# Gram products put into the recurrence's visits, and four inverse steps behind each h, in a DeltaNet and SwiGLU kernel

## The chip, the cores and the metric

The kernel runs on one core of one Trainium2 chip. The metric is the device time of one execution in microseconds (us). The core has five engines that run beside each other and wait for each other through semaphores: PE (matmuls, with its weight loads shown as PEld), DVE (vector work), ACT (activations and copies), POOL (a few general operations) and SP (it issues most DMAs).

## The reference

Two parts, one behind the other, all in float32. The first is a delta rule over 4 batches and 8 heads, 768 tokens, head size 48:

```python
k_n = k / (np.linalg.norm(k, axis=-1, keepdims=True) + 1e-06)
for t in range(S):
    kt, vt, bt = (k_n[:, :, t], v[:, :, t], beta[:, :, t, None])
    y[:, :, t] = np.einsum('bhd,bhde->bhe', q[:, :, t], state)
    v_old = np.einsum('bhde,bhd->bhe', state, kt)
    state = state + bt[:, :, :, None] * np.einsum('bhd,bhe->bhde', kt, vt - v_old)
```

Then y, as 3072 tokens of 384 numbers, goes through a SwiGLU block with d_ff = 1536: `(silu(x @ w_gate) * (x @ w_val)) @ w_out`.

## The kernel before

**Chunks and stages.** The 768 tokens are cut into 12 chunks of 64. The recurrence (chunk c needs the state that chunk c-1 left) and the FFN run at the same time: while PE works on the FFN of chunk c, the small matmuls of chunk c+1's recurrence are put between its big ones. The FFN of one chunk from chunk 2 on is called *stage c* here. It consists of six gate/value pairs (`gate_val`, f = 0, 2, ..., 10; line 847: 6 matmuls of p_gate, 6 of p_val, on full 128 x 128 tiles) and of the output product (from chunk 3 = `FAST` on `output_fast`, line 959, which saves one of eight quarter products by sums and differences of h). After each pair ACT makes silu, DVE multiplies it into h (line 862), and in the later three pairs `sums_of_h` (lines 917 and 944) makes sums of rows that the output product reads.

**The recurrence of a chunk** is `advance(c)`, in four steps: (1) v scaled, then p_r = kt x state, p_y = qt x state, and v minus p_r on DVE (line 759); (2) p_u = inverse x v, copied to uu by ACT; (3) p_s, the new state (added on DVE, line 803), and p_y completed, copied to y; (4) p_f, the transposition of y for the FFN. Steps 1 to 3 use 64 x 64 tiles, in groups of 64 rows of the trace.

**Its preparation** is made ahead. `turned(c, of_q)` transposes k or q of a chunk on DVE (kt, qt, line 422) and sends for the next chunk's blocks by DMA. `gram` multiplies them (line 444); DVE copies the k gram to a_sb and the masked q gram to p_sb. When both k grams of a pair g of chunks (2g, 2g+1) are there, `invert(g)` is entered in a list `fills`. It is a sequence of small DVE steps: three transposes of mb (lines 477, 480), a power on POOL (line 655) during which the sequence yields `WAIT` twice, some scaling, 31 substitution steps of two dependent instructions each (lines 510 and 516), and transposes into zt and z1. `join(g)` completes the inverse with two products on PE with 32 x 32 tiles (lines 706 and 720), with ACT and DVE copying between and behind.

**Order.** The program order of each engine is written out by the kernel's own Python loops, and each engine works its queue in that order:

```python
        for c in range(2, NCH):
            for f in range(0, FT, 2):
                point(c + 1)
                gate_val(c, f, fill)
            point(c + 1)
            ...
                output_fast(c, fill)
            ...
            finish(c + 1)
```

`point` is a place for a *visit*: a run of small-tile matmuls between the big ones. Before, it takes either a step of `advance`, or, in `prep_step`, a join step, or the transposes of the next chunks, or, one point later, their grams (`products`: k of one chunk and q of another in one visit). `fill(n)` runs n steps of the list `fills`: 2 behind p_gate, 3 behind each h, and 2, 2 and 7 within and behind the output product.

**PSUM.** The pair tags "px" and "py" hold one two-bank tile each, for all of the recurrence; the tag "ffn" has four banks, which p_gate, p_val and p_o take in turn.

## Time and profile before

| | us |
|---|---|
| median of 8 runs | 738.91 (738.03 to 741.15) |
| the profiled execution | 739.28 |
| its span on the core | 737.6 |
| PE busy, DVE busy | 698.0, 472.9 |
| stage 4 (305.6 to 362.6) | 57.0 |
| stage 5 (362.6 to 416.6) | 54.0 |

A profile's row gives a start in us from the span's start, a duration, the engine, the source line, and what is written from what, with partitions x elements; a number in brackets is the engine's idle time before it and what ended it. Matmuls overlap, so the distance from one start to the next is what a group costs. Up to about 205 us the kernel also converts the FFN's weights on DVE; behind that the stages repeat in pairs, the even ones with an inverse and the odd ones without. The granted clock over the span was 0.968, and 1.00 in the stages.

### The profile page before, as it was taken

What the parts mean: (1) busy time and instruction counts of PE and PEld (TensorE: products, weight loads), DVE (VectorE), ACT (ScalarE), POOL (GpSimd) and SP (SyncE); (2) the same over time, 40 slices, a digit from 0 to 9 for tenths busy, and PEclk for the clock granted to TensorE, in tenths of its full rate; (3) what the DMA queues carried; (4) which work ended last, traced back from release to release, by engine and by line L of the source; (5) the groups of instructions that cost most, each with busy time, mean ns of one, the idle gap of its engine ahead of it and who ended that gap; (6) DMA issues with size and microseconds to landing.
All of it is one profiled execution on the core that took longest, in us unless ns stands there. A gap on an engine that the chain in (4) does not pass through costs nothing.

```text
span 737.6 us, 22478 instructions
## 1 busy us (share of the span) xinstructions
PE 698.0 (95%) x10132; PEld 605.0 (82%) x10132; DVE 472.9 (64%) x977; ACT 154.6 (21%) x287; POOL 66.4 (9%) x46
## 2 busy tenths in 40 slices
PE   4748899999999999999999999999999999999997
PEld 3636788866787788988988988988988988989987
DVE  5999988978498163678854678854578853313122
ACT  3555444302401112011012011012011012021010
POOL 7008100201200000030000030000030000000000
PEclk9556999999999999999999999999999999999999
DMA  7775444121231012331302331302310100100000
GB/s 149 188 222 139 124 108 127 39 40 24 56 43 26 22 24 42 48 67 14 53 3 46 42 58 26 52 3 38 48 28 12 33 3 3 23 3 0 22 1 21
DMA packets 130735, 37.18 MB, mean 50 GB/s; under 512 B 122864, under 2 KB 125936, under 8 KB 130640
## 3 DMA queue, kind: packets, MB, share of 16 engines
q1 hardware_dynamic: 127184, 34.01, 23.0%
q10 hardware_dynamic: 3072, 1.57, 1.0%
q8 instruction: 79, 1.29, 0.7%
q0 software_dynamic: 384, 0.17, 0.2%
q14 instruction: 16, 0.13, 0.1%
HBM read 31.01 MB, written 4.72 MB: 48 GB/s over the span
## 4 chain that ended last, share of the span: by engine, by line
PE 82%; DVE 14%; issue 1%; DMA 1%; ACT 0%; SPq 0%; ACTq 0%; DVEq 0%
PE p_gate L847 23%; PE p_val L847 23%; PE p_o L959 17%; PE p_o L876 6%; DVE tmp L510 3%; PE p_g L444 3%; DVE zb L516 3%; PE p_u L763 2%; PE p_r L742 1%; PE p_s L794 1%; PE p_y L782 1%; PE p_y L751 1%; DVE last_h L287 1%; DMA kn<-in_k_dram 1%; DVE h_f L862 1%
## 5 line engine op out<-in xcount | busy, mean ns | idle before, releaser
L847 PE MATMUL p_gate<-x_ffn,wg_sb 128*128 128x256 f32 x864 | 205.3, 388 | 1.5 <-ACT x_ffn L830 1.5
L847 PE MATMUL p_val<-x_ffn,wv_sb 128*128 128x256 f32 x864 | 198.5, 379 | 0.0
L847 PEld LDWEIGHTS p_val<-x_ffn,wv_sb 128*128 128x128 f32 x864 | 163.8, 190 | 22.3
L847 PEld LDWEIGHTS p_gate<-x_ffn,wg_sb 128*128 128x128 f32 x864 | 161.6, 192 | 24.4 <-ACT x_ffn L830 2.0
L862 DVE TENSOR_TENSOR h_f<-sil,p_val 128x512 f32<-128x512 f32 x71 | 48.5, 683 | 147.6 <-PE p_val L847 147.2
L856 ACT ACTIVATE sil<-p_gate 128x512 f32<-128x512 f32 x72 | 43.0, 597 | 277.3 <-PE p_gate L847 251.1
L655 POOL TENSOR_TENSOR n_b<-mb,half 128x32 f32<-128x32 f32 x5 | 43.3, 8662 | 409.4 <-DVE mb L480 368.2
L959 PE MATMUL p_o<-wo_sb,h_f 128*128 128x192 f32 x432 | 75.6, 328 | 0.1
L959 PEld LDWEIGHTS p_o<-wo_sb,h_f 128*128 128x128 f32 x432 | 70.3, 190 | 1.2 <-DVE o_sb L969 0.7
L510 DVE TENSOR_TENSOR tmp<-zb,mb 128x31 f32<-128x31 f32 (+15 forms) x186 | 63.2, 340 | 12.1 <-PE p_j L630 6.8
L516 DVE TENSOR_TENSOR zb<-zb,tmp 128x31 f32<-128x31 f32 (+15 forms) x186 | 63.7, 342 | 6.6 <-DVE tmp L510 0.2
L969 DVE TENSOR_TENSOR o_sb<-o_sb,p_o 128x192 f32<-128x192 f32 x45 | 15.7, 349 | 53.4 <-PE p_o L959 36.2
L876 PE MATMUL p_o<-wo_sb,h_f 128*128 128x384 f32 x136 | 45.7, 490 | 0.0
L876 PEld LDWEIGHTS p_o<-wo_sb,h_f 128*128 128x128 f32 x136 | 25.4, 190 | 16.5
L959 PE MATMUL p_o<-last_k,h_f 128*128 128x192 f32 x180 | 32.2, 326 | 0.0
L959 PEld LDWEIGHTS p_o<-last_k,h_f 128*128 128x128 f32 x180 | 29.7, 190 | 0.0
L917 DVE TENSOR_TENSOR h_f<-h_f,h_f 128x256 f32<-128x256 f32 x54 | 22.4, 424 | 8.0 <-PE p_o L959 7.1
L959 PE MATMUL p_o<-last_h,h_f 128*128 128x192 f32 x144 | 26.3, 326 | 0.0
L959 PEld LDWEIGHTS p_o<-last_h,h_f 128*128 128x128 f32 x144 | 23.9, 190 | 0.0
L254 ACT ACTIVATE last_h<-last_h,rebias 128x512 int32<-128x512 uint32 (+2 forms) x26 | 15.3, 616 | 30.5 <-DVE last_h L246 30.5
L763 PEld LDWEIGHTS p_u<-vin,zt 64*64 64x64 f32 x768 | 13.7, 141 | 6.9 <-issue 3.2
L763 PE MATMUL p_u<-vin,zt 64*64 64x48 f32 x768 | 15.7, 228 | 2.4 <-DVE vin L759 1.2
(180 smaller groups left out, 689.2 us busy)
## 6 DMA issues: line engine op xcount, KB each, us to landing
vin<-in_v_dram SPq DMA_DIRECT2D x96, 48.0 KB
kn<-in_k_dram SPq DMA_DIRECT2D x40, 96.0 KB
out_dram<-o_sb SPq DMA_DIRECT2D x36, 96.0 KB
zt<-in_moe_w_out_dram SPq DMA_DIRECT2D x6, 384.0 KB
staged<-in_moe_w_out_dram SPq DMA_DIRECT2D x6, 384.0 KB
qpad<-in_q_dram SPq DMA_DIRECT2D x36, 64.0 KB
wo_sb<-in_moe_w_gate_dram SPq DMA_DIRECT2D x4, 512.0 KB
wo_sb<-in_moe_w_val_dram SPq DMA_DIRECT2D x4, 512.0 KB
```

The costliest lines, as they stand in the source:

```text
L444: nc.tensor.matmul(p_v[par][half_of(b if of_q else b ^ par), bp, j], kt[c][half_of(par), bp, j, b], xt[half_of(par), bp, j, b],)
L510: nc.vector.tensor_tensor(out=t_v, in0=zb[:, 0 : j + 1, j : j + 1].to_broadcast([128, j + 1, m]), in1=mb[:, j : j + 1, j + 1 : R].to_broad ...
L516: nc.vector.tensor_tensor(out=zb[:, 0 : j + 1, j + 1 : R], in0=zb[:, 0 : j + 1, j + 1 : R], in1=t_v, op=ALU.add,)
L655: nc.gpsimd.tensor_tensor(out=n, in0=mb.rearrange("p j i -> p (j i)")[:, 0 : R * R : R + 1], in1=half, op=ALU.pow,)
L763: nc.tensor.matmul(p_u[half_of(b), par, bp, j], zt[half_of(b ^ par), par, bp, j], r[half_of(b ^ par), par, bp, j], start=first, stop=True, ...
L847: nc.tensor.matmul(ps[name][:, i], w_sb[:, t, (f + i) * 128 : (f + i + 1) * 128], xts[c][:, t], start=(t == 0), stop=(t == KT - 1),)
L856: nc.scalar.activation(sil, ps[name], ACTF.Silu)
L862: nc.vector.tensor_tensor(out=hs[c, f], in0=sil, in1=ps["p_val"], op=ALU.mult)
L876: nc.tensor.matmul(p_o, hs[c, f - f % 2][:, f % 2, bp * 128 : (bp + 1) * 128], wo_sb[:, f], start=(f == 0), stop=(f == FT - 1),)
L917: nc.vector.tensor_tensor(out=out, in0=a, in1=b, op=ALU.subtract)
L959: nc.tensor.matmul(p[x, part], a(f - f % 2)[:, f % 2], b(f), start=not begun and f == 0, stop=f == FH - 1, skip_group_check=True,)
L969: nc.vector.tensor_tensor(out=out, in0=a, in1=b, op=ALU.add)
```

## The change

Three things change. In `advance` the product p_y moves from step 1 to step 2, ahead of p_u, for all chunks, and step 1 ends with the subtraction. `fill` behind each h takes four steps instead of three from stage 3 on. And from chunk 4 of the recurrence on (`c > 3` in `point`) a new function `merged` replaces the choice in `point`: it goes through a fixed order of places in each stage, namely (0) transposes of one k and one q, (1) p_r with a gram behind it in the same visit (k for an odd chunk, q for an even one), (2) the first join product with the k gram behind it (even chunk) or the q gram alone (odd chunk), (3) the second join product (even chunk only), (4) p_y and p_u, (5) p_s and p_y, (6) p_f. Place 2 of an even chunk is guarded: it is left empty, and tried again at the next point, until the inverse has been finished before an earlier point. The first join product takes an "ffn" bank instead of "px".

```diff
@@ join
-        p_j = ps_pair("p_j", "px")[:, 0].rearrange("p (c m i) -> p c m i", c=2, m=M)
+        p_j = ps_ffn([128, 512], "p_j").rearrange("p (c m i) -> p c m i", c=2, m=M)
@@ advance
         r = vin.pop(c)
-        p_y = recur(ps_pair("p_y", "py"))
         if c > 0:
             p_r = recur(ps_pair("p_r", "px"))
...
+            nc.vector.tensor_tensor(out=r, in0=r, in1=p_r, op=ALU.subtract)
+        yield
+        p_y = recur(ps_pair("p_y", "py"))
+        if c > 0:
             for bp, j, par, b, first in every():
                 nc.tensor.matmul(
                     p_y[half_of(b ^ par), par, bp, j],
...
-            nc.vector.tensor_tensor(out=r, in0=r, in1=p_r, op=ALU.subtract)
-        yield
         p_u = recur(ps_pair("p_u", "px"))
@@ gate_val
-        fill(3)
+        fill(3 if c < FAST else 4)
@@ new, and point and finish
+    stage_of, seen = {}, set()
+
+    def merged(c):
+        if c >= NCH:
+            return
+        at, k_c, q_c = stage_of.get(c, (0, None, None))
+        g = c // 2
+        ready = c % 2 == 1 or g in seen
+        seen.update(inverted)
...
+        def gram_k(tag):
+            if k_c is not None:
+                gram(k_c, False, tag, (nc.vector.tensor_copy,) * 2)
+                if k_c % 2 == 1:
+                    fills.append((k_c // 2, invert(k_c // 2)))
+
+        if at == 0:
...
+            if k_of and steps("advance", freed_by_k(k_of[0])) >= 4:
+                k_c = k_of.pop(0)
+                turned(k_c, False)
+            if q_of and q_of[0] == c:
+                q_c = q_of.pop(0)
+                turned(q_c, True)
+        elif at == 1:
+            a_step()
+            if c % 2 == 1 and k_c is not None:
+                gram_k("py")
+            else:
+                gram(q_c, True, "py")
+                if c % 2 == 1:
+                    at = 3
+        elif at == 2:
+            if not ready:
+                return
+            if c % 2 == 0:
+                if steps("join", g) < 1:
+                    step("join", join, g)
+                gram_k("px")
+            else:
+                gram(q_c, True, "px")
+                at = 3
+        elif at == 3:
+            if steps("join", g) < 2:
+                step("join", join, g)
+        elif at < 7:
+            a_step()
+        stage_of[c] = (at + 1, k_c, q_c)
+
     def point(c):
+        if c > 3:
+            merged(c)
+            return
...
     def finish(c):
-        if c < NCH:
+        if c > 3:
+            while c < NCH and steps("advance", c) < 4:
+                if stage_of.get(c, (0,))[0] == 2 and c % 2 == 0 and c // 2 not in inverted:
+                    fill_some(1000)
+                merged(c)
+        elif c < NCH:
```

## The prediction

> **What bounds the kernel now.** I read the page's first section and chain first, then the windows by stage, then the timeline of one pair of stages for PE and for DVE. (Stage n is the FFN of chunk n: six gate/value pairs and the output product.)

> ```profile
> PE 698.0 (95%) x10132; PEld 605.0 (82%) x10132; DVE 472.9 (64%) x977; ACT 154.6 (21%) x287; POOL 66.4 (9%) x46
> ...
> PE 82%; DVE 14%; issue 1%; DMA 1%; ACT 0%; SPq 0%; ACTq 0%; DVEq 0%
> ```

> PE sets the time, yet 14% of the chain runs on DVE. The windows (span, then busy time of PE, PEld, DVE, ACT, POOL) show where after the start-up. The first two are stages 4 and 5, one pair:

> ```profile
> 305.60:362.60 57.00, 55.97 (x811) 50.31 (x811) 46.66 (x96) 7.24 (x13) 7.34 (x3) 1.00 0.33 50
> 362.60:416.60 54.00, 54.00 (x812) 48.41 (x810) 27.83 (x50) 8.84 (x15) 0.00 (x0) 1.00 0.13 25
> ...
> 527.70:583.30 55.60, 54.57 (x748) 49.34 (x748) 44.30 (x93) 7.24 (x13) 7.34 (x3) 1.00 0.20 31
> ```

> In the even stages 4, 6 and 8, which hold an inverse, DVE is busy 46.7 of 57.0 us and PE has gaps; in the odd ones PE has none. PE's timeline:

> ```profile
> 346.25 1.16 PE L444 MATMUL p_g<-kt 64*64 64x64 f32 x64 [0.93 <-DVE kt L422]
> ...
> 367.80 2.75 PE L847 MATMUL p_gate<-x_ffn,wg_sb 128*128 128x256 f32 x12
> 370.39 2.75 PE L847 MATMUL p_val<-x_ffn,wv_sb 128*128 128x256 f32 x12
> 373.08 1.29 PE L706 MATMUL p_j<-zt,a_sb 32*32 32x32 f32 x128
> 374.29 2.86 PE L847 MATMUL p_gate<-x_ffn,wg_sb 128*128 128x256 f32 x12
> 376.99 2.75 PE L847 MATMUL p_val<-x_ffn,wv_sb 128*128 128x256 f32 x12
> ...
> 386.27 1.15 PE L742 MATMUL p_r<-state,kt 64*64 64x48 f32 x64
> 387.23 1.11 PE L751 MATMUL p_y<-state,qt 64*64 64x48 f32 x64
> 388.28 2.86 PE L847 MATMUL p_gate<-x_ffn,wg_sb 128*128 128x256 f32 x12
> ```

> From start to start: p_gate or p_val between its like takes 2.59 us, p_val ahead of a visit (a run of small-tile matmuls) 2.68, p_gate behind one 2.69. A visit of one group of 64 takes 1.08 (p_u), of two 0.97 + 1.04 = 2.01, the join's 32-tile group 1.22. Two visits of one group thus cost 2 x (1.08 + 0.19) = 2.54 us, one visit of two 2.01 + 0.19 = 2.20: **a visit saved is worth 0.34 us**. p_f (0.65) has no edges.

> The other loss is PE waiting for DVE. DVE's timeline around that gap:

> ```profile
> 343.20 0.43 DVE L510 TENSOR_TENSOR tmp<-zb,mb 128x255 f32<-128x255 f32 x1
> ...
> 344.95 1.25 DVE L422 STREAM_TRANSPOSE kt<-qpad 128x1024 f32<-128x1024 f32 x1
> 346.12 1.20 DVE L422 STREAM_TRANSPOSE qt<-qpad 128x1024 f32<-128x1024 f32 x1
> ...
> 348.92 0.68 DVE L862 TENSOR_TENSOR h_f<-sil,p_val 128x512 f32<-128x512 f32 x1
> 349.63 0.42 DVE L944 TENSOR_TENSOR h_f<-h_f,h_f 128x256 f32<-128x256 f32 x1
> ```

> And POOL's timeline, the power in the same inverse, for which the substitution waits:

> ```profile
> 316.34 6.20 POOL L655 TENSOR_TENSOR n_b<-mb,half 128x32 f32<-128x32 f32 x1 [126.92 <-DVE mb L480]
> ```

> The transposes stand behind the substitution; the grams (L444) wait for them. Pair 4/5 takes 416.63 - 305.59 = 111.04 us. In it p_val ahead of the gap lasts 3.69 instead of 2.68 (1.01 lost), the grams 2.31 instead of 2.02 (0.29), the output product behind them 14.06 instead of 13.75 (0.31, where L969 at 360.17 comes late): **1.61 us of waits**. Pair 6/7 loses the same. Pair 8/9, whose second visit holds one gram, loses 1.12. Together 4.34 us.

> **The change: visits.** The order of the built programs shows no matmul more or fewer; PE's visits in stages 3 to 10 fall from 40 to 35 (6, then six times 5, then 4, become 5, 4, 5, 4, 5, 4, 5, 3). 5 x 0.34 = **1.7 us gained**. Splitting p_r from p_y in chunks 1 to 3 costs nothing: the count of visits stays, and p_u still waits for the subtraction where DVE's queue sets it (90.58 in chunk 1). The two visits that put a 32-tile group ahead of a 64-tile group are not in this trace; between a join alone (1.22) and a p_r with a follower (0.97 against 1.08, so 0.11 less) I take 0.1 either way each. The first join product now takes an FFN bank, so the p_gate behind it takes the bank that h of f=2 reads: by DVE's sums below that h is done 0.8 us ahead or more. No cost, and at most some tenths if that cover went. DMA loads are issued behind the moved transposes, now once a stage (54 us apart, 40 at the closest before), stores ahead of them: nothing waits.

> **Where DVE ends up in an even stage.** Times from the stage's first p_gate (0). Before, the k gram was visited at 0 and the substitution began at 326.14 - 305.59 = 20.6. Now the gram comes behind f=0 and p_r, at 5.27 + 0.97 = 6.24. DVE starts h of f=0 at 5.45 (0.18 behind p_val, as at 400.29), then v's scaling and subtraction (0.95 each), two gram copies (0.68 each), two transposes (2.14, 2.13), h of f=2 at 13.5, the third transpose (2.16) to 16.3. POOL's power takes 6.20, to 22.6; from there to the first step are 3.56 (322.58 to 326.14): **substitution from 26.2, 5.7 later than before**. Against this, the next chunk's transposes (2.4) and gram copies (2.6) have left the stretch, and six steps a pair instead of five use DVE's idle time (1.86 us at 334.41 before).

> To h of f=10 the queue holds 16 steps (0.45 us at 31 elements to 0.92 at 256, as in the rows: 12.1), two groups of h and sums (1.86 each) and the state's sum (0.95); less 0.12 at each of five changes between independent work (DVE starts such an instruction 0.08 before the last ends, a dependent one 0.03 behind it), 16.2: h starts at 42.4, the second sum ends 1.6 later, at 44.0. PE, not held up, starts the output product at 39.6 and reaches the matmuls that read this sum 1.95 + 1.30 later, at 42.85: **a wait of 1.2 us**. Behind it stand 8 steps (6.9), two adds, three differences (L917) and the add that frees p_o: from h 10.3, to 52.75. PE needs it at 52.6; its last part then takes 2.05, and the stage ends at 54.85. Without waits it would be 6 x 5.18 + 4 x 0.19 + 7.11 + 0.65 + 13.65 = 53.25. So **1.6 us**, three times.

> **The odd stage behind it.** 0.48 us for the last add, seven steps (4.16), kt 1.17, qt 1.20: the q gram can start at 7.05, PE is there at 6.24: **0.8 us**, in stages 5 and 7 (stage 9 has no kt and no wait). PE runs in order, so the whole FFN stands behind either wait. What is late next has cover: the first h comes 6 us late, but its bank is needed over 4 us after that; the join finds its transposes done 3 us early or more; p_y finds the q gram's bank emptied 1.5 us early in the even stages. The guard skips one visit place in stages 5, 7 and 9; p_f then falls inside the output product, at no cost.

> **The sum.** Visits -1.7; old waits gone -4.34; new ones 3 x 1.6 + 2 x 0.8 = 6.4. Total +0.36. The profiled execution took 739.28 us (span 737.6): 739.6. It lies 0.37 above the median of the runs, so the median goes from 738.91 to 739.3.

> [...] The rows show the overlap of 0.08. If all 19 changes of work between substitution and last add lost it (0.11 each), the sum would be 3 x 2.1 us higher, 745.6; nothing above uses this.

> **Rivals.** *Faster:* DVE is not late and the new waits stay away: -1.7 - 4.34, 732.9; if only the output product's waits go, 739.3 - 4.8 = 734.5. For it: the steps moved forward fill real idle time, and 1.6 us earlier suffices. Against it: every row in the queue repeats within 0.02 us from stage to stage. *Slower:* the inverse starts later still. All DVE work behind POOL's power shifts with it, and the output product ends as much later, three times; from 0.4 us later it passes the bound. The group's mean of 8.66 us in place of 6.20 would make 3 x 2.46 = 7.4 us, 746.7; 1 us makes 742.3. Against it: only the first of five powers is long (18.5 us at 58), the others are 6.20 to 6.21. *No effect:* if the guard or the banks left the old order there would be no difference; the built order speaks against it.

> **Numbers.** Forecast 0.56: 739.3, its own range 737.9 to 741.0 (0.35 us a stage in DVE's sum, three times, and the unseen tile changes). Faster rival 0.18, slower rival 0.24, no effect 0.02. A measurement can tell about 0.2%, 1.5 us, from no change. Of the forecast 0.46 lie within that, 0.08 above, 0.02 below: faster 0.20, same 0.48, slower 0.32. The range leaves out the far halves of the rivals: 734.5 to 742.8.

> **What would show it.** Right: in the windows by stage, even stages near 54.9 and odd ones near 56.6 (54.8 for stage 9); no idle PE before a k gram; a wait of p_o for DVE's sums (L917 or L944) near 1.2 us, of the q gram for qt near 0.8; substitution from 26 us into the stage. Wrong: even stages at 53.3 (faster rival), or a power that ends past 23 us into the stage (slower one).

## The result and the profile after

The changed kernel takes 741.52 us (median of 13 runs, 740.04 to 742.92) against 738.72 before (35 runs): a ratio of 1.0035, interval 1.0028 to 1.0043. It is slower by 2.8 us, where 739.3 was forecast. The profiled execution took 741.25 us with a span of 739.5.

The page, with the lines that answer to those of before:

```profile
PE 698.2 (94%) x10132; PEld 605.3 (82%) x10132; DVE 473.7 (64%) x977; ACT 154.3 (21%) x287; POOL 63.4 (9%) x46
...
PE 73%; DVE 16%; issue 3%; POOL 2%; SPq 2%; ACT 1%; DMA 1%; DVEq 0%; ACTq 0%
```

The same instructions, PE as busy as before. In the chain of the work that ended last, PE's share falls from 82% to 73%, and "issue", time for which the profile shows no cause, rises from 1% to 3%. The windows of stages 4 to 9 (span, busy time of PE, PEld, DVE, ACT, POOL, granted clock, DMA share, GB/s) say where:

```profile
304.40:358.60 54.20, 53.85 (x684) 48.15 (x684) 43.73 (x90) 7.25 (x13) 6.58 (x3) 1.00 0.25 39
358.60:415.60 57.00, 56.10 (x939) 50.51 (x938) 31.02 (x56) 8.77 (x15) 0.00 (x0) 1.00 0.23 36
415.60:469.60 54.00, 53.82 (x684) 48.13 (x683) 43.81 (x90) 7.25 (x13) 6.58 (x3) 1.00 0.25 39
469.60:530.60 61.00, 58.16 (x941) 51.98 (x940) 31.03 (x56) 8.74 (x15) 0.00 (x0) 0.97 0.21 34
530.60:584.60 54.00, 53.77 (x683) 48.08 (x683) 43.86 (x90) 7.25 (x13) 6.58 (x3) 1.00 0.15 24
584.60:639.50 54.90, 54.90 (x877) 49.50 (x876) 28.62 (x53) 8.76 (x15) 0.00 (x0) 1.00 0.10 16
```

| stage | 3 | 4 | 5 | 6 | 7 | 8 | 9 | 10 |
|---|---|---|---|---|---|---|---|---|
| predicted after | 54.85 | 54.85 | 56.65 | 54.85 | 56.65 | 54.85 | 54.8 | 51.0 |
| measured after | 54.86 | 54.17 | 57.06 | 54.00 | 60.95 | 54.06 | 54.85 | 51.10 |

The prediction states the even stages, "near 56.6" for 5 and 7, and 54.8 for stage 9. For 5 and 7 the table has the old pair's 111.04 less its waits (1.61), one visit (0.34) and the even stage without waits (53.25), plus the new wait of 0.8; for 3 and 10 it has the stages of before (55.19 and 51.34) less one visit. Seven stages lie within 0.9 us of this. Stage 7 lies 4.3 above, though it holds the same instructions as stage 5. Stages 3 to 10 together grew by 441.05 - 438.20 = 2.85 us; the span of the profiled execution grew by 2.0 only, because its start-up, which differs from one execution to the next, was 0.86 us shorter. PE's waits from stage 3 to stage 10 (total, times, longest):

```profile
PE p_g L444 <- issue: 1.9, 1, 1.9
PE p_g L444 <- DVE qt L422: 1.8, 2, 0.9
PE p_o L960 <- DVE h_f L918: 0.7, 3, 0.3
```

The second and third are the two waits of the prediction. The first was not in it. PE's timeline, first around the predicted wait of stage 5, then around the other in stage 7:

```profile
363.84 1.15 PE L741 MATMUL p_r<-state,kt 64*64 64x48 f32 x64
365.89 1.16 PE L444 MATMUL p_g<-qt,kt 64*64 64x64 f32 x64 [0.90 <-DVE qt L422]
...
488.61 1.29 PE L706 MATMUL p_j<-zt,a_sb 32*32 32x32 f32 x128
489.83 0.97 PE L444 MATMUL p_g<-kt 64*64 64x64 f32 x49
492.73 0.46 PE L444 MATMUL p_g<-kt 64*64 64x64 f32 x15 [1.93 <-issue]
493.11 4.54 PE L848 MATMUL p_gate<-x_ffn,wg_sb 128*128 128x256 f32 x12
497.50 2.75 PE L848 MATMUL p_val<-x_ffn,wv_sb 128*128 128x256 f32 x12
```

A k gram stops in its middle, after 49 of 64 matmuls. Its operands and its bank were good enough for the first 49, so it hardly lacks DVE or a bank; the experiments test this. Then p_gate takes 4.39 from start to start instead of 2.69. The windows around it (the column before the DMA share is the granted clock) tell why:

```profile
490.00:493.50 3.50, 1.57 (x66) 1.39 (x63) 0.95 (x2) 0.79 (x2) 0.00 (x0) 1.00 0.03 7
493.50:497.00 3.50, 3.50 (x10) 2.79 (x9) 1.03 (x2) 0.00 (x0) 0.00 (x0) 0.51 0.02 5
497.00:500.00 3.00, 3.00 (x15) 2.51 (x14) 0.00 (x0) 0.60 (x1) 0.00 (x0) 1.00 0.00 0
```

Behind the stop PE ran some 3.4 us at half clock. Together, stop and half clock make 60.95 - 57.06 = 3.9 us. What PE lacked can be seen in the DMA view of 488 to 494 (40 slices of 0.15 us):

```profile
GB/s 0 0 0 0 0 0 0 0 0 0 0 0 0 109 0 55 0 0 0 0 0 0 0 0 0 0 0 0 0 0 0 0 0 0 0 0 0 0 109 0
...
q8 instruction: 2, 0.03, 2.6%
```

and in the page's list of queues:

```profile
q8 instruction: 79, 1.29, 0.7%
```

By the page, queue 8 carries nothing but instructions: 79 transfers of 1.29 MB / 79 = 16 KB. (The 55 in slice 15 is another queue's, q14.) PE has 2 x 10132 = 20264 rows, a row being one matmul or one weight load. That makes one transfer per 256 rows, 64 bytes a row, so I take queue 8 to bring PE's instructions. The transfer of slice 13 (490.0) is recorded until 491.28; PE had stopped at 490.80. Counting rows, PE had then run some 386 beyond a multiple of 256; in the slow stretches, transfers start as early as 81 rows beyond one (65 in the kernel before). So PE seems to ask for the next 256 rows some 70 rows into a block (an estimate from these starts), and can run 316 more meanwhile (386 less 70). At p_gate's pace (48 rows in 5.2 us) these last over 30 us. The merged visit has 256 rows of the join in 1.22 us and 128 of the gram in 1.1: 384 rows in 2.3 us. In stage 7 the asking, which I call the fetch point, fell 38 rows into that visit; in stage 5, 206.

### The profile page after: what moved, and what is told of

Read it like the earlier page. It is cut to its first block, busy times and chain, and to the rows that moved or that the text cites. A ratio compares the mean times of both kernels' runs of the same rounds, so it can differ in the third digit from the quotient of the medians.

```text
span 739.5 us, 22467 instructions
## 1 busy us (share of the span) xinstructions
PE 698.2 (94%) x10132; PEld 605.3 (82%) x10132; DVE 473.7 (64%) x977; ACT 154.3 (21%) x287; POOL 63.4 (9%) x46
## 3 DMA queue, kind: packets, MB, share of 16 engines
q8 instruction: 79, 1.29, 0.7%
## 4 chain that ended last, share of the span: by engine, by line
PE 73%; DVE 16%; issue 3%; POOL 2%; SPq 2%; ACT 1%; DMA 1%; DVEq 0%; ACTq 0%
PE p_gate L848 22%; PE p_val L848 21%; PE p_o L960 16%; DVE tmp L510 3%; DVE zb L516 3%; PE p_g L444 3%; POOL n_b L655 2%; PE p_o L877 2%; DVE mb L480 2%; PE p_y L783 1%; PE p_u L764 1%; DVE h_f L863 1%; SPq L120 1%; PE p_s L795 1%; PE p_y L754 1%
## 5 line engine op out<-in xcount | busy, mean ns | idle before, releaser
L655 POOL TENSOR_TENSOR n_b<-mb,half 128x32 f32<-128x32 f32 x5 | 39.5, 7908 | 420.2 <-DVE mb L480 379.0
L510 DVE TENSOR_TENSOR tmp<-zb,mb 128x31 f32<-128x31 f32 (+15 forms) x186 | 63.4, 341 | 12.3 <-PE p_j L630 6.8
L877 PEld LDWEIGHTS p_o<-wo_sb,h_f 128*128 128x128 f32 x136 | 25.4, 190 | 16.5
L775 ACT COPY uu<-p_u 128x768 f32<-128x768 f32 (+1 forms) x13 | 9.6, 749 | 40.4 <-PE p_u L764 40.4
```

The source lines that it names most:

```text
L510: nc.vector.tensor_tensor(out=t_v, in0=zb[:, 0 : j + 1, j : j + 1].to_broadcast([128, j + 1, m]), in1=mb[:, j : j + 1, j + 1 : R].to_broad ...
L655: nc.gpsimd.tensor_tensor(out=n, in0=mb.rearrange("p j i -> p (j i)")[:, 0 : R * R : R + 1], in1=half, op=ALU.pow,)
L877: nc.tensor.matmul(p_o, hs[c, f - f % 2][:, f % 2, bp * 128 : (bp + 1) * 128], wo_sb[:, f], start=(f == 0), stop=(f == FT - 1),)
```

## The experiments

**Theory A**: the stop is PE without instructions, and it depends on where a fetch point falls in the visit of 384. **Rivals**: B, the gram waits for DVE, a bank or data unseen; C, the change from 32- to 64-row tiles in one visit costs it. Apart from these stand the prediction's own terms: the two DVE waits, the visits, and each half of the change.

### The same program, 100 and 176 PE instructions later

Matmuls of the start-up's k gram of chunk 3 are issued again, 25 of them (the kernel shift25) or 44 (shift44), four PE rows each:

```diff
+        for bp, j, par, b, _ in (list(every()) * 2)[: AGAIN.get((c, of_q), 0)]:
+            nc.tensor.matmul(
+                p_v[par][half_of(b if of_q else b ^ par), bp, j],
+                kt[c][half_of(par), bp, j, b],
+                xt[half_of(par), bp, j, b],
+            )
```

> The changed kernel with 25 matmuls of one k gram of the start-up issued a second time (same operands, same results): 100 more PE instructions (25 matmuls of two passes, each with a weight load) long before the stages in question, nothing else. Theory A (PE runs out of fetched instructions in the visit of 384 instructions in stage 7, because a fetch of 256 instructions is asked for some 38 instructions into it and lands after the stock is used up): 100 instructions more move that point to about 62 instructions ahead of the visit, and the one of stage 5 from 206 to 106 instructions into its visit; both then have enough in stock. The stop of 1.93 us and the slow p_gate behind it go, stage 7 takes 57.1 instead of 60.95, the whole 737.6 (737.0 to 738.4). Theory B (the k gram waits for DVE, a bank or data by a way that the profile does not show): nothing moves, stage 7 stays at 60.95 and the whole at 741.5, plus at most 0.4 for the added matmuls. Theory C (the change of tile from 32 to 64 costs it): as B, and it would show in stage 5 too.

Measured: stage 5 at 57.07, stage 7 at **57.08** (60.95 before the shift), span 735.8 instead of 739.5; median 738.47 (737.31 to 741.81), ratio to before 1.0006 (0.9994 to 1.0019). 25 superfluous matmuls make the kernel 3 us faster, in the median. Stage 7 in PE's timeline:

```profile
488.73 1.29 PE L714 MATMUL p_j<-zt,a_sb 32*32 32x32 f32 x128
489.94 1.16 PE L446 MATMUL p_g<-kt 64*64 64x64 f32 x64
491.04 2.86 PE L856 MATMUL p_gate<-x_ffn,wg_sb 128*128 128x256 f32 x12
```

> The same with 44 matmuls issued a second time, 176 instructions. Theory A: the point of stage 7 moves out of reach (138 instructions ahead of the visit), that of stage 5 moves to 30 instructions into its visit, so the stop moves from stage 7 to stage 5, after about 45 of the 64 passes of the k gram (346 instructions into the visit), 1.8 to 2.0 us long, followed by a slow p_gate or not: stage 7 at 57.1, stage 5 at 59.0 to 61.0, the whole as the changed kernel, 740.0 to 742.5. Theories B and C: stage 5 stays at 57.06 and stage 7 at 60.95.

Measured: stage 5 at **60.72**, stage 7 at 57.08; median 741.69, ratio 1.0044 (1.0028 to 1.0060). The stop has moved to stage 5, to 48 matmuls into the gram, with the half clock behind it:

```profile
379.08 0.93 PE L446 MATMUL p_g<-kt 64*64 64x64 f32 x48
381.74 0.46 PE L446 MATMUL p_g<-kt 64*64 64x64 f32 x16 [1.73 <-issue]
382.13 4.11 PE L856 MATMUL p_gate<-x_ffn,wg_sb 128*128 128x256 f32 x10
```

B and C fall: operands, banks, tiles and order are the same in all three kernels; only the count of instructions ahead differs. That the stock of instructions is what ran out follows from the place to which the stop moved. In all fourteen traces of this case, "issue" stops of this kind behind the start-up are three: after the change, here, and in the kernel with merged visits and three steps below. They come 387, 392 and 387 rows past a multiple of 256, and they are the only places behind the start-up where a fetch's recorded end comes later (by 0.6 to 0.7 us) than row 386 past its multiple.

### The k gram in a visit of its own

```diff
                 if steps("join", g) < 1:
                     step("join", join, g)
-                gram_k("px")
...
+        elif at == 7 and c % 2 == 0:
+            gram_k("px")
```

> The changed kernel with the even chunk's k gram taken out of the visit of the first join product and put alone between two parts of the output product. Theory A: no visit has more than 256 instructions, no stop; one visit more in stages 5 and 7 (0.34 us each by the prediction's price): stage 5 at 57.4, stage 7 at 57.4, the whole 738.2 (737.6 to 739.0). Theory B (the gram itself waits): the stop goes with the gram into the output product, 741.5 or more. DVE's two copies of the gram (0.68 each) then stand ahead of the last two adds of the output product, where DVE is idle in an odd stage: no wait expected.

Measured: stage 5 at 57.28, stage 7 at 57.27, span 736.3, median 738.00, ratio 1.0004 (0.9991 to 1.0018). No stop: the fetch points lie where they lay after the change, but no visit holds more than 256 rows. The extra visit costs 57.28 - 57.07 = 0.2 a stage. This kernel, called late_k, is the base of what follows.

### Each half of the change alone

Merged visits with three steps (`fill(3)` in place of `fill(3 if c < FAST else 4)`):

> The changed kernel with three inverse steps behind each h again (half of the change alone). The order of the programs: the join comes one visit later in stages 5, 7 and 9, six steps fewer stand ahead of the output product, and the next chunk's transposes stand four steps (1.7 us) ahead of the inverse's end. If the prediction's waits are right, the output product's wait for DVE's sums (0.7 to 0.9) goes in stages 4, 6, 8 and the q gram's wait for qt (1.08) in stages 5 and 7: 4.5 us gained; the join is a visit (5.2 us) later and does not wait. Theory A: the fetch point in stage 7 lies about 10 instructions ahead of the visit, a stop of about 1 us there instead of 1.93: the whole 734 to 736.5. Rival (the fourth step is what keeps the inverse in time): the join waits or the last visits fall behind the output product, 741.5 or more.

Measured: 743.75, ratio 1.0070 (1.0056 to 1.0084). The output product's wait is gone (even stages 53.32), as expected. But the q gram waits longer, not less (2.0 in stages 5 and 7, 0.8 in stage 9, which had no such wait), and stage 7, at 61.84, has its stop:

```profile
PE p_g L444 <- DVE qt L422: 4.7, 3, 2.0
PE p_g L444 <- issue: 1.9, 1, 1.9
```

In PE's timeline the stop is

```profile
497.13 0.62 PE L444 MATMUL p_g<-kt 64*64 64x64 f32 x25
499.63 0.81 PE L444 MATMUL p_g<-kt 64*64 64x64 f32 x39 [1.88 <-issue]
```

It comes 256 + 50 = 306 rows into the visit, where a fetch point 10 rows ahead of it puts the end of the stock; its length was expected at about 1 us. My expectation forgot the `fill(7)` behind the output product: seven steps stand ahead of the transposes however many came before, and now they are the longer ones of the triangle. The fourth step costs 0.7 to 0.85 us in each even stage and saves 0.9 to 1.1 in each odd one.

The kernel before with the fourth step only:

> The kernel before with the fourth inverse step alone. By the order of the programs the join comes one visit earlier and the next chunk's grams come inside the output product instead of behind it; visits are not fewer. The steps fill idle DVE time in the even stages, so the gram's wait for the transposes behind the substitution (1.61 us a pair) should shrink: 735 to 738. Rival: with six more steps ahead of the sums of h the output product waits (as after the change, 0.7 to 0.9 a stage), or the grams, now 5 us earlier, wait longer: 739 to 743. I hold the second likelier, since the grams move forward by more than the steps do.

Measured: **757.33**, ratio 1.0252 (1.0238 to 1.0266); the rival's direction, not its size. The old `prep_step` takes what is ready, so joins and grams come a visit earlier; that this puts them out of step with DVE is my reading of the order, not tested by itself. The kernel's largest waits for DVE (one of the three on L759, 1.2, stood there before):

```profile
PE p_g L444 <- DVE kt L422: 6.2, 2, 3.2
...
PE p_u L763 <- DVE vin L759: 4.3, 3, 1.5
...
PE p_g L444 <- DVE qt L422: 3.3, 1, 3.3
```

Three intervals of 3.4 us at half clock come with these waits (one at 347 us, two at 576). With the old order the fourth step does not pay here.

### The two predicted waits, one at a time (on late_k)

The last seven steps behind the next chunk's transposes (turn_first):

```diff
         store(c, 0, o[0])
-        fill(7)
...
                 point(c + 1)
+                if f == 0 and c > FAST:
+                    fill(7)
                 gate_val(c, f, fill)
```

> On the kernel late_k (stages 5 and 7 at 57.28 each, profiled span 736.3): the seven inverse steps behind the output product are moved behind the next chunk's transposes of kt and qt. Prediction's theory (the q gram waits 1.08 for the transpose of qt, which stands behind the last seven steps): the transposes end 2.9 us into the stage instead of 7.3, the wait goes in stages 5 and 7, 56.2 each; the steps move 2.4 us back and the inverse's transposes keep their place, so the join has its data as before. Whole: 2.2 less than late_k, span 734.1, median 735.8. Rival (the wait is only handed on: the first h, the join or p_u becomes late): 57.3, no gain.

Measured: 736.77, ratio 0.9979 (0.9968 to 0.9990); stages 5 and 7 at 56.80, less than half of the gain that was expected. The q gram's wait is gone, and over half of it comes back behind the join, where p_gate needs the bank from which DVE makes h of f=2:

```profile
PE p_gate L848 <- DVE h_f L863: 1.2, 2, 0.6
PE p_o L960 <- DVE h_f L918: 0.8, 3, 0.4
```

The odd chunk's gram copies on ACT, so that DVE begins the inverse earlier (act_copies):

```diff
-                gram(k_c, False, tag, (nc.vector.tensor_copy,) * 2)
+                copies = (nc.scalar.copy if k_c % 2 else nc.vector.tensor_copy,) * 2
+                gram(k_c, False, tag, copies)
```

> On late_k: the two copies of the odd chunk's k gram (0.64 each on DVE), for which the inverse's first transpose stands in line, are made on ACT, so DVE begins the inverse 1.3 us earlier. Prediction's theory (stages 4, 6 and 8 lose 0.7 to 0.9 each because DVE's queue from the power on ends too late for the output product): all three waits go, stages at 53.3 instead of 54.1, and the q gram's wait in stages 5 and 7 shrinks by what the inverse gains beyond that, about 0.4 each: span 733 to 734, median 735. Rival (the power or another step sets the begin; ACT's copies end as late as DVE's did): under 0.5 gained.

Measured: 736.49, ratio 0.9974 (0.9964 to 0.9985). Stages 4, 6 and 8 at 53.65, 0.4 to 0.56 less, but 0.35 above the 53.3 that was expected. The substitution begins 24.8 us into stage 4 instead of 25.4: DVE's 1.3 us of copies became 0.48 of waiting for ACT's. The q gram's wait stays 0.9, since the even stage ends earlier by about as much as the inverse.

### POOL's power beside DVE

```diff
+            for i in range(4):
+                spare = work.tile([128, 256], FP32, name="tmp", bufs=1)
+                nc.vector.tensor_tensor(
+                    out=spare, in0=m_f[:, 0:256], in1=m_f[:, 256:512], op=ALU.mult
+                )
         yield WAIT
```

> On late_k: four DVE products of 128x256 with both inputs in SBUF, results unused (0.42 each, 1.7 us), stand in DVE's queue where it waits for POOL's power. Before the change the power took 6.20 with v's scaling (0.96, both inputs in SBUF) beside it, after it 5.44 with none beside it. If that scaling is what made it longer (0.76 for 0.96), the power now takes 5.44 + 1.7 x 0.79 = 6.8; the substitution begins 1.3 us later, and by the prediction's rival the output product of stages 4, 6 and 8 ends 1.3 later: three times 1.3 = 4, span 740.3, median 742. If the power's time has another cause: 5.44 and no change, as DVE is idle there.

Measured: 739.89, ratio 1.0019 (1.0010 to 1.0029). The power takes 5.67, not 6.8;

```profile
321.51 1.80 DVE L665 TENSOR_TENSOR tmp<-mb 128x256 f32<-128x256 f32 x4
```

is DVE's line in stage 4, and POOL's is

```profile
321.55 5.67 POOL L655 TENSOR_TENSOR n_b<-mb,half 128x32 f32<-128x32 f32 x1 [133.78 <-DVE mb L480]
```

Where the same four begin 0.05 *behind* the power, in stage 1 of this trace, it takes 5.44, with v's scaling (L401) in its middle too:

```profile
179.94 5.44 POOL L655 TENSOR_TENSOR n_b<-mb,half 128x32 f32<-128x32 f32 x1 [36.38 <-DVE mb L480]
179.99 1.88 DVE L665 TENSOR_TENSOR tmp<-mb 128x256 f32<-128x256 f32 x4
...
181.79 0.95 DVE L401 TENSOR_TENSOR vin<-vin,n_t 128x768 f32<-128x768 f32 x1
```

So the lengthening is not in proportion to what runs beside it. It fits these cases that only an instruction with both inputs in SBUF, begun just *ahead* of the power, holds it up, for its own length less 0.2: 0.96 - 0.20 = 0.76 before the change (6.20; v's scaling began at 316.29, the power at 316.34), 0.42 - 0.19 = 0.23 here. After the change the instruction in that place is the q mask product (one input in PSUM) and the power takes 5.44. These rows show a hold-up at the start only; the first power of all, 18.48 us before the change and 17.01 after it, at 58 us, while DVE converts weights, is not explained by this. The price of a late inverse comes out in the sum, though not stage by stage: the substitution began 0.22 to 0.26 later, and stages 4, 6 and 8 grew by 0.08, 0.44 and 0.21, which is 0.73 or three times 0.24. Another 0.65 of the profiled span arose ahead of stage 4, where the first of these inverses holds the four products too.

### Putting them together

First late_k with ACT's copies, the transposes first, and the seven steps behind the stage's first h (the kernel best, so called ahead of its run):

```diff
                 gate_val(c, f, fill)
+                if f == 0 and c > FAST:
+                    fill(7)
```

> late_k with ACT's copies of the odd k gram and with the next chunk's transposes ahead of the last seven inverse steps, these steps now behind the first h of the stage, so that this h does not come late as in turn_first (where p_gate waited 0.58 for it). Theory (the waits are DVE's queue, and each goes where its cause is taken away): stages 4, 6, 8 at 53.65 as in act_copies, stages 5 and 7 at 57.28 - 1.08 = 56.2, span 736.3 - 3 x 0.5 - 2 x 1.08 = 732.6, median 734.3. Rival (waits are handed on again): odd stages at 56.8, span 733.8, median 735.5.

Measured: **744.29**, ratio 1.0077 (1.0063 to 1.0090): neither theory's number. Even stages 53.65 as expected; stages 5 and 7 at 59.69 and 59.43. DVE stood idle 1.2 us ahead of the first h with the steps behind it; h of f=2 comes that much later still, and p_gate behind the join waits, long enough for the half clock (4.38 us from its start to p_val's):

```profile
375.46 1.29 PE L706 MATMUL p_j<-zt,a_sb 32*32 32x32 f32 x128
378.54 4.54 PE L848 MATMUL p_gate<-x_ffn,wg_sb 128*128 128x256 f32 x12 [1.79 <-DVE h_f L863]
```

Then the same with 21 matmuls issued a second time (best_aligned), and this with the k gram back in the join's visit (merged_aligned):

> best with 21 matmuls of the start-up's k gram issued a second time (84 instructions). From the trace of late_k the shortest time in which PE runs the 316 instructions between the asking for a fetch and the end of the stock is then 5.4 us instead of 3.6. If fetches that come late in some executions make the runs differ by 2 to 4 us, the runs now lie within 1.5 us of each other, the median at best or up to 0.5 lower; if the differences come from elsewhere (the clock of the start-up), the spread stays and the median is that of best plus up to 0.3.

Measured: 743.65 (742.87 to 745.49), ratio 1.0073 (1.0060 to 1.0086). The spread of 2.6 us (3.2 in best) did not shrink to the 1.5 expected, which speaks against late fetches as what makes runs of one kernel differ. What does is left open, and it is as large as the effects here: five of shift25's eleven runs (739.4 to 741.8) and three of late_k's eleven (740.8 to 741.6) lie 1 to 4 us above the rest, which end at 738.5 and 738.2. The kept trace of each is of a run of the lower group.

> As best_aligned, but with the even chunk's k gram left in the visit of the first join product as the change has it. The 84 instructions put the fetch points of stages 5 and 7 at 122 instructions into and 46 ahead of the visit of 384. Theory A: no stop in either stage; against best one visit less in stages 5 and 7, measured as 57.28 - 57.07 = 0.2 each: span 732.2, median 733.9. If the visit of 384 instructions starves wherever the points lie: 735 or more.

Measured: 738.79, ratio 1.0007 (0.9998 to 1.0015), not the 733.9 of theory A. No stop in stages 5 and 7 (56.73, 56.72): the visit of 384 runs through when its fetch points lie well, and the gram in it covers 1.1 us of p_gate's wait. Stage 9, whose visit holds the join alone, has the wait of 1.8 and the half clock (58.41 instead of 54.86).

Last, the two edits that had gained, in the form in which they gained:

> The two edits that each gained, together and in the form in which they gained: late_k with ACT's copies of the odd k gram and with the transposes ahead of the last seven steps, the steps ahead of the stage's first p_gate again as in turn_first. Theory (the gains are separate: the copies act on the even stages, the transposes on the odd ones): stages 4, 6, 8 at 53.65, stages 5 and 7 at 56.8, where p_gate behind the join waits 0.6 for h of f=2; span 733.7, median 735.4, below both act_copies and turn_first. Rival (the shorter even stage leaves the odd one the inverse's end later, as in best, and p_gate's wait grows beyond 1 us and may bring the half clock): 737 or more.

Measured: **736.20** (735.27 to 736.98), ratio 0.9968 (0.9956 to 0.9980), span 734.0. Stages 4, 6, 8 at 53.64; 5 and 7 at 56.82 and 56.81: the gains add. It is faster than the kernel before by 2.5 us and than the changed one by 5.3. Of the waits that the view lists one is left:

```profile
PE p_gate L848 <- DVE h_f L863: 1.2, 2, 0.6
```

## Why the prediction was right or wrong, step by step

- **The range held, the forecast's own did not.** 741.52 lies in 734.5 to 742.8 but above 741.0. That it lies in the range is luck: 2.3 us too much for the output product's waits hid part of 3.9 us for something that had no term. A difference of 1.5 us was to count as a change; by that the kernel is slower, to which the prediction gave 0.32, and 0.48 to "same".
- **Visits, right.** Stage 3 went from 55.19 to 54.86, stage 10 from 51.34 to 51.10, a visit each; the price of 0.34 was 0.2 to 0.33. "Splitting p_r from p_y in chunks 1 to 3 costs nothing": from p_gate to p_gate, stages 1 and 2 (chunks 2 and 3 of the recurrence) took 76.03 and 57.58 us against 76.09 and, less the join's visit at the end, 57.68 before.
- **Old waits, right.** The k gram waits for DVE's transposes no more; the 4.34 are gone.
- **The output product's wait, mechanism right, size wrong.** "Substitution from 26.2": it began 329.82 - 304.40 = 25.4 into stage 4. "POOL's power takes 6.20" is the failed term: the row of before was lengthened by v's scaling that began 0.05 ahead of it,

```profile
316.29 0.96 DVE L401 TENSOR_TENSOR vin<-vin,n_t 128x768 f32<-128x768 f32 x1
```

  and the change puts that scaling elsewhere. What now begins 0.05 ahead of the power reads PSUM, and the power takes

```profile
320.73 1.29 DVE L459 TENSOR_TENSOR p_sb<-p_g,mask_q 128x512 f32<-128x512 f32 x2
320.78 5.44 POOL L655 TENSOR_TENSOR n_b<-mb,half 128x32 f32<-128x32 f32 x1 [132.09 <-DVE mb L480]
```

  0.76 us less, and so the three waits, by the prediction's 53.25, are 0.75 to 0.92 instead of 1.6.
- **The q gram's wait, right.** Predicted 0.8, measured 1.08, twice; turn_first took it away where the prediction placed it.
- **"The two visits that put a 32-tile group ahead of a 64-tile group ... 0.1 either way", wrong question.** The tile change costs nothing (1.22 + 1.09 in stage 5). What counts is how many instructions the visit packs into how little time: this is the step that failed, a cost put at next to nothing that was 3.9 us (stop and half clock) in stage 7. Nothing in the trace of before shows a stop of this kind, but it does show queue 8, 79 transfers and the pace of the rows, from which a visit of 384 rows in 2.3 us could have been set against a transfer's time (1.02 us as recorded there, at the median).
- **"What is late next has cover", half right.** It held for the change as made. The cover of p_gate's bank behind the join was in part the q gram's wait itself: turn_first lost 0.6 to it, best 1.8.
- **The slower rival's price, right in the sum; its mechanism did not occur.** The inverse came 0.8 earlier than forecast, not later; when it was made 0.22 to 0.26 later, the three stages lost 0.73.
- **DVE's overlap, right.** Its loss, weighed in the prediction at 2.1 us for each even stage, did not occur: in stage 4 h of f=10 starts at 346.17, the step ahead of it ends at 346.26, and the step behind the sums starts 0.09 before the last of them ends (348.02 against 348.11). The output product's waits differ from the forecast by the power's 0.76 and nothing came on top.

Summed: +0.36 predicted; even stages -2.3, stages 5 and 7 +0.8, stop and half clock +3.9, which makes 2.8. Stages 3 to 10 grew by 2.85.

## What to carry to other kernels

Merging small-tile matmuls saves their edges (0.2 to 0.3 us here), but count the instructions: where 384 of them run in 2.3 us, PE can outrun its instruction supply, and whether it does depends on how many instructions stand ahead of it (modulo 256 here; stage 7 took 60.95 us, and 57.08 with 100 more ahead). A visit of 256 never did so here. A wait in an in-order queue is also cover for what comes behind it (0.6 us in turn_first, 1.8 in best): before taking it away, work out which buffer is late next. And a duration taken from one row holds for that row's neighbours (6.20 or 5.44 us for the same power here): see what begins just ahead of it on the other engines before using it for a new order.

## What the hardware showed that I had not expected

```profile
477.70:481.20 3.50, 3.50 (x69) 3.02 (x63) 3.29 (x9) 0.00 (x0) 0.00 (x0) 0.51 0.65 87
...
500.50:504.00 3.50, 3.50 (x17) 3.09 (x18) 1.28 (x2) 0.60 (x1) 0.00 (x0) 1.00 0.02 5
```

  So 1.73 us idle, about half an interval, was enough here. The stops of 1.7 to 1.9 us cost 1.95 to 2.2 us by themselves (from the gram's start to the next p_gate), and 3.65 to 3.9 with the 1.7 of a half-clock interval.
- **POOL held up at its start.** The same power took 6.20 us where v's scaling (0.96, both inputs in SBUF) began 0.05 ahead of it, 5.67 where a product of 0.42 (both inputs in SBUF) began 0.04 ahead, and 5.44 where the q mask product (1.29 for two, one input in PSUM) began 0.05 ahead.
